# Preparing an output weight early, through memory, in an adaLN attention and gMLP kernel

## The chip, the cores and the metric

The kernel runs on one core of a Trainium2 chip. The metric is the time of one execution on the device in microseconds (us); of several runs the median counts. A core has five engines that work side by side, each through its own instructions in order: TensorE (PE, matrix products into the accumulators in PSUM; its weight loads are shown as PEld), VectorE (DVE), ScalarE (ACT), GpSimd (POOL) and SyncE (SP), which here only issues transfers between the chip's memory and the on-chip buffer SBUF. Transfers are carried out by 16 DMA engines. An engine or a queue that waits for something holds up all that stands behind it in its own order.

## The reference

A block with 2048 tokens of width 448, 16 heads of 28, and a hidden half-width of 896; all in float32:

```python
mod = (silu(c) @ w_mod).reshape(6, 448)          # sa, ca, ga, sb, cb, gb
h = layernorm(x) * (1 + ca) + sa
x = x + ga * attention(h, wqkv) @ wo             # 16 heads, softmax
h = layernorm(x) * (1 + cb) + sb
z = gelu(h @ w_in)                               # 2048 x 1792
z1, z2 = z[:, :896], layernorm(z[:, 896:])
g = w_sp @ z2 + b_sp[:, None]                    # mixing over the 2048 tokens
x = x + gb * ((z1 * g) @ w_out)                  # w_out: 896 x 448
```

The gate `gb` multiplies the columns of `w_out`'s result, so it can be multiplied into `w_out` beforehand.

## The kernel before

Matrix products that need more precision than one pass gives are done with operands split in two: a high part, which is the value rounded to the type float32r, and a low part, the value minus the high part. Three products (high by high, high by low, low by high) then stand for one. So each weight has to be split before it is used, one copy (high) and one subtraction (low) per block.

The work goes in stages: modulation, first layer norm and projections; attention; the attention's output projection and second layer norm; `z1` (first half of the hidden width, stored to memory); `z2`; mixing with the output projection laced into its end; the rest of the output projection.

**Attention.** A loop over 256 slots `u` (16 heads of 16 key blocks). Each slot issues four score matmuls and their exponentials (ScalarE), four matmuls for the row maxima of a later head (20 slots ahead) with their VectorE reductions, and, every other slot, the products with V of the two slots before. Side work is put into slots with `at(slot, fn, ...)`: in each slot first its events run in the order in which they were registered, then the matmuls, then the events in `late`. For each head there are loads of its q and k (`load_head`, SP, some 30 slots ahead of the head's first), the row of maxima (`m_fin`: ScalarE and GpSimd produce two rows, SP writes them into place; four slots before the head), and for finished heads the division and scatter of the result (`n_copy` to `n_scatter`). Other events prepare later work. `ws_load`, `ws_add` and `ws_store` form 80 sums of blocks of `w_sp` and store them, up to slot 187. `wo_load` and `wo_prep` do `wo`, from slot 120, with buffers of the pool `stage2` (two buffers under the tag `ql`). `win_first` loads half of `w_in` from slot 200.

**Mixing.** The product with `w_sp` is done with sums of blocks, in four phases p = 0 to 3 of two halves with eight steps each. A step is 21 matmuls in phases 0 to 2 and 12 in phase 3. For a step, `w_load` (SP, two to three steps ahead) loads one or two blocks of weights into `raw_sp` (four buffers), and `w_split` (one to two steps ahead) splits each: high part by ScalarE (L994), low part by VectorE (L84, the line of the helper `sub`). The matmuls are L1106 to L1108. At the end of each half, `evac` empties the accumulators with VectorE and ScalarE (L1112 is the VectorE addition). The function `extras(p, half, st)` adds the side work of a step; it is called one step later, after the loads and splits and ahead of the matmuls. The stationary operands of phases 0 to 2 lie in `heapA` (steps 0 to 3) and `heapB` (steps 4 to 7); those of phase 3 in `heapA` and the last columns of `heapB`, split from z2 by `prep3` (L1003).

**w_out.** Its seven blocks of 128 rows are prepared from step 3 of phase 2's second half to step 4 of phase 3's first half. `wout_load` loads a block into a buffer of the tag `x2t` (two buffers, L1189) and GpSimd multiplies it by the gate (L1190); `wout_part` makes the high part with ScalarE (L1194) and the low part with VectorE (L84), into the first 6272 columns of `heapB`, as these come free, and then calls `wout_load` for the block two further on. The output matmuls (`y_part`, L1212 to L1214) begin with the first step of phase 3's second half.

Of the kernel before, what the change touches and what calls it, by code (L numbers as in the profile page):

```python
# [8 lines left out]
F32 = mybir.dt.float32  # L9
F32R = mybir.dt.float32r  # L10
AF = mybir.ActivationFunctionType
ALU = mybir.AluOpType
# [4 lines left out]
S, D, H, DH, FH = 2048, 448, 16, 28, 896  # L17
# [16 lines left out]
def tile_adaln_mha_gmlp(ctx, tc, x, wqkv, wo, w_in, w_spT, b_sp, w_out, cT, w_mod, out):  # L34
    nc = tc.nc
    ctx.enter_context(tc.manual_schedule())
    pe, dve, act, pool, sp = nc.tensor, nc.vector, nc.scalar, nc.gpsimd, nc.sync
# [3 lines left out]
    scr = ctx.enter_context(tc.tile_pool(name="scr", bufs=1, space=DRAM))  # L41
# [4 lines left out]
    x2_scr = scr.tile([S, D], F32, name="x2_scr")  # L46
    z1_scr = scr.tile([FH, S], F32, name="z1_scr")
    ws_scr = scr.tile([80, 128, 512], F32, name="ws_scr")

    ident = const.tile([128, 128], F32, name="ident")  # L50
    make_identity(nc, ident)
# [8 lines left out]
    bcs = {"gb": const.tile([128, D], F32, name="bc_gb")}  # L60
# [5 lines left out]
    def hview(heap, off, a, b):  # L66
        return heap[:, off : off + a * b].rearrange("p (a b) -> p a b", b=b)
# [15 lines left out]
    def sub(eng, dst, a, hi):  # L83
        eng.tensor_tensor(out=dst, in0=a, in1=hi.bitcast(F32), op=ALU.subtract)  # L84
# [5 lines left out]
    def weight_part(dst, i, raw, hi_eng, lo_eng, zero=True, c0=0):  # L90

        cs = slice(c0, c0 + raw.shape[-1])
        h = dst[:, i if i < 3 else 6, cs]
        if hi_eng is act:
            act.activation(h, raw, AF.Copy)
        else:
            hi_eng.tensor_copy(h, raw)
        if i < 3:
            sub(lo_eng, dst[:, 3 + i, cs], raw, h)
        else:  # L100
            sub(lo_eng, dst[0:64, 7, cs], raw[0:64], h[0:64])
            if zero:
                pool.memset(dst[64:128, 7, cs].bitcast(F32), 0.0)
# [47 lines left out]
    stage2 = att.enter_context(tc.tile_pool(name="stage2", bufs=2, side="right"))  # L151
# [311 lines left out]
    for g in range(1, NG):  # L463
        if g == 3:
# [14 lines left out]
            def load_head(h, c0=0, c1=S):  # L479
                k, q = kst[h % 3], qst[h % 3]  # L480
                if h > 2:
                    sp.dma_start(q[84:86, :].bitcast(F32), q[86:88, :].bitcast(F32))
                for r0, i in ((0, 0), (56, 1), (28, 0)):
                    sp.dma_start(k[r0 : r0 + 28, c0:c1].bitcast(F32), qk_scr[i][D + h * DH : D + (h + 1) * DH, c0:c1])
                for r0, i in ((0, 0), (28, 1), (56, 0)):
                    sp.dma_start(q[r0 : r0 + 28, c0:c1].bitcast(F32), qk_scr[i][h * DH : (h + 1) * DH, c0:c1])
# [159 lines left out]
    def wo_prep(i):  # L646
        pool.tensor_tensor(out=wo_raw[i], in0=wo_raw[i], in1=bcs["ga"], op=ALU.mult)
        weight_part(wos, i, wo_raw.pop(i), pool, pool)

    wraw = []  # L650

    def win_first(i):
# [44 lines left out]
    def at(slot, fn, *a, when=events):  # L697
        when.setdefault(slot, []).append((fn, a))
# [20 lines left out]
    for i in range(4):  # L719
        at(120 + 8 * i, wo_load, i)  # L720
        at(124 + 8 * i, wo_prep, i)
        at(200 + 8 * i, win_first, i)

    load_head(1)

# [273 lines left out]
    def z_sum(dst, a, b, op=ALU.add, eng=pool):  # L999
        eng.tensor_tensor(out=dst, in0=a, in1=b, op=op)  # L1000
# [5 lines left out]
    def prep0(st):  # L1006
        h, l = zst[st][:, 0:896], zst[st][:, 896:1792]
        z_part(h[:, F1], l[:, F1], z2[st][:, F1])
        z_part(h[:, F2], l[:, F2], z2[8 + st][:, F1])
        z_part(h[:, F6], l[:, F6], z2[8 + st][:, F6])  # L1010

    def prep1(st):
        h, l = zst[st][:, 0:896], zst[st][:, 896:1792]
        z_part(h[:, F1], l[:, F1], z2[8 + st][:, F2])
        z_part(h[:, FQ], l[:, FQ], z2[st][:, FQ])

    def prep2(st):
        z_part(zst[st][:, 0:896], zst[st][:, 896:1792], z2[st])
# [44 lines left out]
    t4 = ctx.enter_context(tc.tile_pool(name="t4", bufs=2))  # L1063
# [14 lines left out]
    wouts_h, wouts_l = (hview(heapB, i * 3136, 7, D) for i in range(2))  # L1078
# [4 lines left out]
    def prep3(st):  # L1083
        a, b = z7[st]
        z_part(a[:, 0:384], a[:, 384:768], z2[8 + st][:, F1])
        z_part(b[:, 0:128], b[:, 128:256], z2[8 + st][:, F6])
# [66 lines left out]
    def z1_load():  # L1153
        if nz[0] < len(gates):
            f, tb = gates[nz[0]]
            if tb == 1:
                z1s[f, tb] = wp.tile([128, 512], F32, name="z1l", tag="raw_sp")
            else:
                z1s[f, tb] = t4.tile([128, 512], F32, name="z1")
            sp.dma_start(z1s[f, tb], z1_scr[f * 128 : (f + 1) * 128, tb * 512 : (tb + 1) * 512])  # L1160
            nz[0] += 1

    def b_load(tb):
        bt[tb] = t4.tile([128, 512], F32, name="bt")
        sp.dma_start(bt[tb], b_sp[tb * 512 : (tb + 1) * 512].rearrange("(o n) -> o n", o=1).broadcast_to([128, 512]))

    def gate(n=1):
        for _ in range(n):
            f, tb = gates[nz[1]]
            nz[1] += 1  # L1170
            u = utile(f, tb)
            d_add(u, u, bt[tb])
            d_add(u, u, z1s.pop((f, tb)), ALU.mult)
            z1_load()
# [3 lines left out]
    def u_split(f, tb):  # L1178
        if tb not in uTs:
            uTs[tb] = hview(dpool.tile([128, 8 * 896], F32R, name="uT", tag=f"heapD{tb % 2}"), 0, 14, 512)  # L1180
        uT, u = uTs[tb], utile(f, tb)
        act.activation(uT[:, f, :], u, AF.Copy)
        sub(dve, uT[:, 7 + f, :], u, uT[:, f, :])

    x2t, yps = {}, {}

    def wout_load(f):
        x2t["w", f] = raw = t4.tile([128, D], F32, name="raw_out", tag="x2t")
        sp.dma_start(raw, w_out[f * 128 : (f + 1) * 128, :])  # L1189
        pool.tensor_tensor(out=raw, in0=raw, in1=bcs["gb"], op=ALU.mult)  # L1190

    def wout_part(f):
        raw = x2t.pop(("w", f))
        act.activation(wouts_h[:, f, :], raw, AF.Copy)  # L1194
        sub(dve, wouts_l[:, f, :], raw, wouts_h[:, f, :])
        if f + 2 < 7:
            wout_load(f + 2)

    def x2_load(t):
        if 8 <= t < 12:  # L1200
            x2t[t] = t4.tile([128, D], F32, name="x2t")
        else:
            x2t[t] = wp.tile([128, 512], F32, name="x2l", tag="wsp_l")[:, :D]
        sp.dma_start(x2t[t], x2_scr[t * 128 : (t + 1) * 128, :])
# [15 lines left out]
    def extras(p, half, st):  # L1220
        if p == 0 and half == 0:
            if st < 2:
                prep0(6 + st)
            z_sum(z2[st][:, F2], z2[st][:, F2], z2[8 + st][:, F2], eng=dve)
        if p == 0 and half == 1:
            prep1(st)
        if p == 1 and half == 0:
            z_sum(z2[st][:, F1], z2[st][:, F1], z2[8 + st][:, F2])
            z_sum(z2[st][:, F2], z2[st][:, F2], z2[st][:, F1], ALU.subtract)
            z_sum(z2[8 + st][:, F1], z2[8 + st][:, F1], z2[st][:, F1], ALU.subtract)  # L1230
        if p == 1 and half == 1:
            prep2(st)
            if st == 6:
                b_load(2)
                b_load(3)
                z1_load()
                z1_load()
        if p == 2 and half == 0:
            if st < 6:
                gate()  # L1240
            if st > 4:
                u_split(st - 5, 2)
        if p == 2 and half == 1:
            for i in ((), (0,), (1,), (2, 3), (4, 5), (6,), (), (7,))[st]:
                prep3(i)
            if st in (1, 2, 3, 4):
                gate()
            if 3 <= st < 7:
                u_split(st, 2)
            if st in (3, 4):  # L1250
                wout_load(st - 3)
            if st > 5:
                wout_part(st - 6)
        if p == 3 and half == 0:
            if st < 5:
                wout_part(2 + st)
            if st == 6:
                x2_load(8)
            if st == 5:
                b_load(0)  # L1260
        if p == 3 and half == 1:
            if st < 4:
                gate()
            else:
                if st == 4:
                    b_load(1)
                u_split(st - 1, 3)
                gate(2 if st > 4 else 1)
            if st in (1, 2, 3):
                u_split(st - 1, 3)  # L1270

    nw = [4, 2]
    for n, (p, half, st) in enumerate(steps):
# [13 lines left out]
        if st == 7:  # L1287
            evac(p, half)
    extras(*steps[-1])
    z1_load()  # L1290
    z1_load()
# [44 lines left out]
```

## Time and profile before

| | |
|---|---|
| runs | 1409.55, 1411.18, 1412.63 us; median 1411.18 |
| profiled execution | 1410.07 us, span 1408.0 us, mean granted TensorE clock 1.000 |
| busy share | PE 99%, VectorE 72%, ScalarE 56%, GpSimd 20% |
| DMA | 186.99 MB, mean 133 GB/s |
| attention, from the first score matmul of the loop to the last (L566) | 153.8 to 872.4 us |
| mixing, from the first matmul start (L1106) to the last | 1060.9 to 1348.8 us |

The span runs from the first to the last instruction of the profiled execution. In the rows of the profile, "x <- y" after an operation names what it writes and reads, "x7" is a count of instructions, L is the line in the kernel, and a name in brackets or behind a bar with "<-" is what ended the engine's idle time before the instruction. "SPq" is SyncE's queue. In a timeline row the first number is the start and the second the length in us, and for several instructions in one row the length is that of them all.

### The profile page before, as it was taken

How to read it: one execution, taken by the hardware profiler on the slowest of the kernel's cores; microseconds unless marked ns; L12 is line 12 of the kernel's file. 1: busy time of each engine (PE TensorE's matmuls, PEld its weight loads, DVE VectorE, ACT ScalarE, POOL GpSimd, SP SyncE). 2: the span in 40 equal slices, each digit the busy share in tenths (PEclk: the TensorE clock that was granted, in tenths of full speed). 3: DMA queues.
4: the chain of work that ended last, by engine and by line, in shares of the span. 5: the costliest groups of instructions: out<-in, count | busy, mean ns of one | idle time of the engine just before them, and what ended most of it. 6: DMA issues, size and time to landing. Idle time of an engine off the chain costs nothing.

```text
span 1408.0 us, 20113 instructions
## 1 busy us (share of the span) xinstructions
PE 1393.6 (99%) x7180; PEld 979.8 (70%) x7180; DVE 1010.5 (72%) x1700; ACT 786.8 (56%) x1532; POOL 287.7 (20%) x276
## 2 busy tenths in 40 slices
PE   7999999999999999999999999999999999999998
PEld 6888655555555555555555554988998888887888
DVE  7778888888888888888888860751356655667573
ACT  3623677777677777777667779263234544334210
POOL 3033312221314243313200021100142430001000
PEclk9999999999999999999999999999999999999999
DMA  8564635555555556654422001534103333444453
GB/s 251 160 176 150 196 101 180 165 162 145 165 161 167 159 163 173 185 147 157 125 68 75 21 18 47 185 114 139 53 1 112 112 110 108 144 142 144 151 178 103
DMA packets 98251, 186.99 MB, mean 133 GB/s; under 512 B 16614, under 2 KB 28006, under 8 KB 95606
## 3 DMA queue, kind: packets, MB, share of 16 engines
q1 hardware_dynamic: 95722, 181.87, 42.7%
q10 hardware_dynamic: 2430, 3.84, 0.7%
q8 instruction: 56, 0.92, 0.3%
q14 instruction: 43, 0.35, 0.1%
HBM read 130.42 MB, written 50.45 MB: 128 GB/s over the span
## 4 chain that ended last, share of the span: by engine, by line
PE 93%; DVE 3%; DMA 2%; issue 1%; ACT 1%; POOL 1%; SPq 0%; ACTq 0%; DVEq 0%; POOLq 0%
PE st_ps L566 18%; PE o_ps L581 17%; PE mt L535 17%; PE acc L1107 6%; PE acc L1108 6%; PE acc L1106 6%; PE z_ps L1032 5%; PE z_ps L918 5%; PE pq L293 4%; PE wo_ps L788 3%; PE y_ps L1213 2%; PE y_ps L1212 2%; PE y_ps L1214 2%; PE pv L278 1%; DMA raw_sp<-ws_scr 1%
## 5 line engine op out<-in xcount | busy, mean ns | idle before, releaser
L540 DVE TENSOR_REDUCE pm<-mt 128x1 f32<-128x512 f32 x1024 | 631.4, 681 | 108.5 <-PE mt L535 108.3
L570 ACT ACTIVATE P<-st_ps 128x512 f32<-128x512 f32 x1024 | 512.5, 631 | 150.7 <-PE st_ps L566 150.7
L566 PE MATMUL st_ps<-qst,kst 128*128 128x512 f32 x1024 | 406.5, 408 | 0.5 <-ACT P L570 0.5
L535 PE MATMUL mt<-kst,qst 128*128 128x512 f32 x1024 | 402.6, 393 | 0.1
L566 PEld LDWEIGHTS st_ps<-qst,kst 128*128 128x128 f32 x1024 | 190.9, 187 | 153.7 <-issue 93.9
L581 PE MATMUL o_ps<-P,V 128*32 128x512 f32 x2048 | 247.5, 598 | 0.0
L535 PEld LDWEIGHTS mt<-kst,qst 128*128 128x128 f32 x1024 | 192.6, 188 | 30.7 <-DVE pm L540 2.3
L994 ACT ACTIVATE wsp_h<-raw_sp 128x512 fp32r<-128x512 f32 x112 | 70.2, 631 | 161.2 <-PE acc L1108 102.6
L688 POOL TENSOR_TENSOR ws_raw<-ws_raw 128x512 f32<-128x512 f32 x80 | 103.0, 1288 | 273.2 <-DMA ws_raw<-in_w_spT_dram 261.1
L84 DVE TENSOR_TENSOR wsp_l<-raw_sp,wsp_h 128x512 fp32r<-128x512 f32 x112 | 81.7, 738 | 90.2 <-ACT wsp_h L994 89.3
L581 PEld LDWEIGHTS o_ps<-P,V 128*32 128x32 f32 x2048 | 54.1, 109 | 123.6 <-issue 116.7
L1107 PE MATMUL acc<-wsp_l,heapA 128*128 128x512 f32 x224 | 87.3, 390 | 0.8 <-DVE wsp_l L84 0.8
L1106 PE MATMUL acc<-wsp_h,heapA 128*128 128x512 f32 x224 | 87.5, 390 | 0.2 <-DVE cD L1112 0.2
L1108 PE MATMUL acc<-wsp_h,heapA 128*128 128x512 f32 x224 | 87.2, 389 | 0.0
L1107 PE MATMUL acc<-wsp_l,heapB 128*128 128x512 f32 x174 | 67.7, 389 | 0.0
L1108 PE MATMUL acc<-wsp_h,heapB 128*128 128x512 f32 x174 | 67.7, 389 | 0.0
L1106 PE MATMUL acc<-wsp_h,heapB 128*128 128x512 f32 x174 | 67.7, 389 | 0.0
L293 PE MATMUL pq<-heapD,heapD 128*128 128x512 f32 x196 | 62.4, 392 | 0.0
L1036 DVE BATCH_NORM_STATS2 stz<-z 128x6 f32<-128x448 f32 x32 | 19.9, 625 | 50.4 <-ACT z L1035 29.5
L1106 PEld LDWEIGHTS acc<-wsp_h,heapA 128*128 128x128 f32 x224 | 42.0, 188 | 9.8 <-DVE cD L1112 1.2
L1107 PEld LDWEIGHTS acc<-wsp_l,heapA 128*128 128x128 f32 x224 | 42.0, 188 | 9.7 <-DVE wsp_l L84 1.2
L1108 PEld LDWEIGHTS acc<-wsp_h,heapA 128*128 128x128 f32 x224 | 42.1, 188 | 8.7
(205 smaller groups left out, 1593.7 us busy)
## 6 DMA issues: line engine op xcount, KB each, us to landing
ws_raw<-in_w_spT_dram SPq DMA_DIRECT2D x160, 256.0 KB
ws_scr<-ws_raw SPq DMA_DIRECT2D x80, 256.0 KB
raw_sp<-ws_scr SPq DMA_DIRECT2D x80, 256.0 KB
kst<-qk_scr SPq DMA_DIRECT2D x45, 224.0 KB
qst<-qk_scr SPq DMA_DIRECT2D x45, 224.0 KB
raw_sp<-in_w_spT_dram SPq DMA_DIRECT2D x32, 256.0 KB
qk_scr<-qh SPq DMA_DIRECT2D x28, 256.0 KB
qk_scr<-ql SPq DMA_DIRECT2D x28, 256.0 KB
```

What stands on the lines that cost most here:

```text
L84: eng.tensor_tensor(out=dst, in0=a, in1=hi.bitcast(F32), op=ALU.subtract)
L293: pe.matmul(pq, wqk[:, b, m * 128 : (m + 1) * 128], hT[g][:, a, :], start=j == 0, stop=j == NST - 1)
L535: pe.matmul(mt, qst[h % 3][:, t * 128 : (t + 1) * 128], kst[h % 3][:, kb * 512 : (kb + 1) * 512], start=True, stop=True)
L540: dve.tensor_reduce(out=pms[h][:, t, kb : kb + 1], in_=mt, axis=AX.X, op=ALU.max)
L566: pe.matmul(st, kst[h % 3][:, kt * 128 : (kt + 1) * 128], qst[h % 3][:, qb * 512 : (qb + 1) * 512], start=True, stop=True)
L570: act.activation(p, st, AF.Exp, scale=SCALE)
L581: pe.matmul(otile[h][32 * qb : 32 * qb + 32, :], V[:, kt, h, :], ptiles.pop((u, qb)), start=kt == 0, stop=kt == NT - 1)
L688: pool.tensor_tensor(out=a, in0=a, in1=b, op=SUMS[i // 16][2])
L918: pe.matmul(ps_t, w1[:, b, f * 128 : (f + 1) * 128], h2T[g][:, a, :], start=j == 0, stop=j == NST - 1)
L1106: pe.matmul(acc[i], zh, hi, start=st == 0, stop=False)
L1107: pe.matmul(acc[i], zh, lo, start=False, stop=False)
L1108: pe.matmul(acc[i], zl, hi, start=False, stop=st == 7)
```

## The change

The gate's multiplication and the split of `w_out` move into the attention's loop. For each of the seven blocks, from slot 196 on and six slots apart, SP loads the block into a buffer of `stage2`, three slots later GpSimd multiplies it by the gate, makes the high part with a copy and the low part with a subtraction, and two slots after that SP stores both parts to two arrays in memory. In the mixing, SP loads the 14 parts from there straight into their places in `heapB`, from step 6 of phase 2's second half to step 7 of phase 3's first half, one or two after each step. No other engine takes part there.

```diff
+    wout_scr = [scr.tile([FH, D], F32, name=f"wout_scr{i}") for i in range(2)]
...
+    wout_t = {}
+
+    def wout_raw(f):
+        wout_t[f] = stage2.tile([128, D], F32R, name="wout_l", tag="ql")
+        sp.dma_start(wout_t[f].bitcast(F32), w_out[f * 128 : (f + 1) * 128, :])
+
+    def wout_prep(f):
+        lo = wout_t[f]
+        hi = stage2.tile([128, D], F32R, name="wout_h", tag="ql")
+        pool.tensor_tensor(out=lo.bitcast(F32), in0=lo.bitcast(F32), in1=bcs["gb"], op=ALU.mult)
+        pool.tensor_copy(hi, lo.bitcast(F32))
+        sub(pool, lo, lo.bitcast(F32), hi)
+        wout_t[f] = hi, lo
+
+    def wout_store(f):
+        for scr_i, t in zip(wout_scr, wout_t.pop(f)):
+            sp.dma_start(scr_i[f * 128 : (f + 1) * 128, :], t.bitcast(F32))
...
+    for f in range(7):
+        at(196 + 6 * f, wout_raw, f)
+        at(199 + 6 * f, wout_prep, f)
+        at(201 + 6 * f, wout_store, f)
...
-    def wout_load(f):
-        x2t["w", f] = raw = t4.tile([128, D], F32, name="raw_out", tag="x2t")
-        sp.dma_start(raw, w_out[f * 128 : (f + 1) * 128, :])
-        pool.tensor_tensor(out=raw, in0=raw, in1=bcs["gb"], op=ALU.mult)
-
-    def wout_part(f):
-        raw = x2t.pop(("w", f))
-        act.activation(wouts_h[:, f, :], raw, AF.Copy)
-        sub(dve, wouts_l[:, f, :], raw, wouts_h[:, f, :])
-        if f + 2 < 7:
-            wout_load(f + 2)
+    wout_order = [(0, 0), (0, 1), (0, 2), (0, 3), (1, 0), (1, 1), (1, 2), (1, 3), (0, 4), (0, 5), (0, 6), (1, 4), (1, 5), (1, 6)]
+
+    def wout_load(n):
+        for i, f in wout_order[:n]:
+            sp.dma_start((wouts_h, wouts_l)[i][:, f, :].bitcast(F32), wout_scr[i][f * 128 : (f + 1) * 128, :])
+        del wout_order[:n]
...
-            if st in (3, 4):
-                wout_load(st - 3)
             if st > 5:
-                wout_part(st - 6)
+                wout_load(2)
         if p == 3 and half == 0:
-            if st < 5:
-                wout_part(2 + st)
+            wout_load(1 if st in (1, 2, 3, 4, 5, 6) else 2)
```

## Prediction, made before the changed kernel ran

> **What bounds the kernel now.** I read the page first: busy times, slices, chain of waits. Then the waits of TensorE (PE) alone, which say where it stands still at all; then the timeline around those places, engine by engine, and the waits of SP.
>
> ```profile
> span 1408.0 us, 20113 instructions
> PE 1393.6 (99%) x7180; PEld 979.8 (70%) x7180; DVE 1010.5 (72%) x1700; ACT 786.8 (56%) x1532; POOL 287.7 (20%) x276
> PE wu L220 <- DMA xg<-in_x_dram: 4.5, 1, 4.5
> PE tp L326 <- DVE xn L262: 2.7, 1, 2.7
> PE pv L278 <- DVE hfull L379: 1.4, 1, 1.4
> PE acc L1107 <- DVE wsp_l L84: 0.8, 1, 0.8
> PE st_ps L566 <- ACT P L570: 0.5, 1, 0.5
> PE acc L1106 <- DVE cD L1112: 0.2, 1, 0.2
> ```
>
> The columns of a wait are total us, times, longest. PE is busy 99% of the span, and the 14.4 us in which it isn't (1408.0 - 1393.6) bound what any change that leaves its matmuls alone can bring. The matmuls are left alone here. The first three waits belong to the kernel's start and to lines that the change doesn't touch; what is left for it is small: 0.8 and 0.2 us in the mixing, 0.5 us once in attention.
>
> **What the holes are worth.** Both waits of the mixing stand in the first steps of its last phase, exactly where w_out is prepared now. A wait's length leaves out the matmul stretched beside it, so I measure from start to start:
>
> ```profile
> 1289.41 0.39 PE L1108 MATMUL acc<-wsp_h,heapB 128*128 128x512 f32 x1
> 1289.63 0.39 PE L1106 MATMUL acc<-wsp_h,heapA 128*128 128x512 f32 x1
> 1290.82 0.39 PE L1108 MATMUL acc<-wsp_h,heapA 128*128 128x512 f32 x1
> 1291.44 0.50 PE L1106 MATMUL acc<-wsp_h,heapA 128*128 128x512 f32 x1 [0.24 <-DVE cD L1112]
> 1291.78 0.39 PE L1107 MATMUL acc<-wsp_l,heapA 128*128 128x512 f32 x1
> 1301.09 0.39 PE L1106 MATMUL acc<-wsp_h,heapA 128*128 128x512 f32 x1
> 1302.26 0.50 PE L1107 MATMUL acc<-wsp_l,heapA 128*128 128x512 f32 x1 [0.78 <-DVE wsp_l L84]
> 1302.60 0.39 PE L1108 MATMUL acc<-wsp_h,heapA 128*128 128x512 f32 x1
> ```
>
> The last phase begins at 1289.63 (heapA's turn), and an undisturbed start to start is 0.22 us (1289.41 to 1289.63). Hole A: 0.62 and 0.34 instead of 0.22 each, 0.52 us lost. Hole B: 1.17 and 0.34, 1.07 us lost. Together 1.6 us.
>
> **Part 1: removed from the mixing.** Per block of w_out: one load of 224 KB (SP), one GpSimd multiply, one ScalarE copy, one VectorE subtraction, seven times.
>
> ```profile
> L1190 POOL TENSOR_TENSOR raw_out<-raw_out,bc_gb x7: 1144/1155/1499, 1279.4 to 1307.5; 128x448 f32<-128x448 f32 x7
> L1194 ACT ACTIVATE heapB<-raw_out x7: 561/562/581, 1286.4 to 1309.1; 128x448 fp32r<-128x448 f32 x7
> L84 DVE TENSOR_TENSOR heapB<-raw_out,heapB x7: 611/615/618, 1287.2 to 1309.8; 128x448 fp32r<-128x448 f32 x7
> SPq L1189 <- DVE heapB L84: 17.1, 3, 7.0
> ```
>
> That is 8.5 us of GpSimd, 3.9 of ScalarE, 4.3 of VectorE: beside a PE that is full, worth nothing in themselves. What counts is the order on two queues.
>
> ```profile
> 1287.18 0.62 DVE L84 TENSOR_TENSOR heapB<-raw_out,heapB 128x448 fp32r<-128x448 f32 x1
> 1287.65 0.51 ACT L1003 ACTIVATE heapB<-z 128x384 fp32r<-128x384 f32 x1
> 1287.72 0.68 DVE L1112 TENSOR_TENSOR cE<-cE,acc 128x512 f32<-128x512 f32 x1
> 1295.61 0.33 SPq L1189 DMA_DIRECT2D raw_out<-in_w_out_dram  x1
> 1296.05 1.23 SPq L986 DMA_DIRECT2D raw_sp<-ws_scr  x1
> 1299.88 0.63 ACT L994 ACTIVATE wsp_h<-raw_sp 128x512 fp32r<-128x512 f32 x1 [7.67 <-DMA raw_sp<-ws_scr]
> 1300.51 1.15 POOL L1190 TENSOR_TENSOR raw_out<-raw_out,bc_gb 128x448 f32<-128x448 f32 x1 [0.79 <-DMA raw_out<-in_w_out_dram]
> 1300.55 1.65 DVE L84 TENSOR_TENSOR wsp_l<-raw_sp,wsp_h 128x512 fp32r<-128x512 f32 x1 [3.82 <-ACT wsp_h L994]
> L84 DVE TENSOR_TENSOR wsp_l<-raw_sp,wsp_h x14: 676/692/1654, 1269.3 to 1309.2; 128x512 fp32r<-128x512 f32 x14
> ```
>
> Hole A: PE waits for a PSUM bank that VectorE's evacuation (L1112, from 1287.72) has not emptied. The subtraction for w_out's first block stands right ahead of it in VectorE's order, from start to start 0.54 us. Without it the evacuation moves up by 0.54, the hole's 0.52 closes. It could move further only if the split ahead of it did.
>
> Hole B has two causes in a row. SP sat on wout_load until VectorE freed raw_out's buffer (17.1 us in three waits, one of 7.0), and the mixing weights' own load (raw_sp, L986) stood behind it until 1296.05; it reached ScalarE at 1299.88, which had idled 7.67 us for it. Then VectorE's subtraction took 1.65 us beside GpSimd's multiply, which began 0.04 us before it; the median of the 14 such rows around is 0.69, so 0.96 too long. Either cause alone nearly makes the hole. Both go: the new loads write heapB and need no VectorE or GpSimd, only that the old phase's matmuls have read those columns. Waits go by columns, not by the whole buffer: ScalarE writes heapB (L1003) at 1287.65, while PE reads other columns of it up to 1289.41. The columns of the first four high parts were last read in step 4 of the old phase's second half; three steps of 21 matmuls at 0.23 follow it, so it ended 14 us before 1289.6, near 1275, and SP gets to these loads at about 1282. So SP is held by raw_sp's own buffers only, and I cost the waits of the new loads at nothing; were they held to the end of that phase (1289.6), the next raw_sp would land 4.2 us later (ScalarE's 1284.65 behind SP's 1280.49, below) and be split in 0.63 + 0.69, by 1295.2, and the step that needs it, the fourth of the phase, begins at 1298.4 (one step, 12 x 0.22, ahead of 1301.09): still nothing.
>
> What made that row 1.65 us long could speak against the change, which moves GpSimd's work beside another VectorE stage. The Trainium skill, SBUF — State Buffer, section "SBUF: two separate sides", says GpSimd and a two-input VectorE instruction on SBUF exclude each other for a whole instruction. The 1.65 us row agrees. By that rule VectorE's attention work, which reads PSUM, is not held and the sum stays -1.6. The Trainium skill, Perfetto Trace Analysis, section "Optimizing Scalar/DVE Operations", warns without that limit that moving work between the two may not help; by it the third rival below would hold.
>
> **Part 2: added to the mixing.** Fourteen loads of 224 KB instead of seven, 3.2 MB (14 x 229 KB in decimal) for 1.6. Issue on SP: 14 x 0.33 us by L1189's row above, 4.6 us for 2.3, in a queue that mostly waits. Traffic:
>
> ```profile
> 1280.00:1285.00 5.00, 5.00 (x24) 4.14 (x23) 3.62 (x6) 2.74 (x6) 1.66 (x2) 1.00 0.76 255
> 1280.49 1.59 SPq L986 DMA_DIRECT2D raw_sp<-ws_scr  x3
> 1284.65 1.29 ACT L994 ACTIVATE wsp_h<-raw_sp 128x512 fp32r<-128x512 f32 x2 [2.17 <-DMA raw_sp<-ws_scr]
> ```
>
> The first row's columns: stretch, its length, busy PE, PEld, DVE, ACT, POOL (instructions), granted clock, DMA share, GB/s. The clock is full and 255 GB/s pass. A last-phase step is 12 matmuls, 2.7 us; one raw_sp (262 KB) and one w_out part (229 KB) per step are 182 GB/s, so the queue keeps up. The tightest place is the three raw_sp issued at 1280.49, which VectorE must split ahead of the evacuation. Today a w_out load goes just ahead of them (1.02 MB, 4.0 us at 255, ScalarE started after 4.16). In the new kernel that one is gone and two follow: 1.25 MB if all share alike, 4.9 us, with an issue some 0.5 us earlier. Bounds on hole A: from closed (in order) to an evacuation 0.9 - 0.5 = 0.4 us later for this and 0.54 earlier for the subtraction, 0.14 in all, so 0.38 of the 0.52 left. I take closed, since the loads are issued in order. The last two parts are issued ahead of the second half's first step, and the output matmuls that read them come after 36 matmuls, 7.9 us, even if SP runs no further ahead than PE; a load takes 4.2: nothing.
>
> **Part 3: added to attention.** Per block on GpSimd a multiply, a copy, a subtraction; on SP one load and two stores.
>
> ```profile
> L647 POOL TENSOR_TENSOR wo_raw<-wo_raw,bc_ga 128x448 f32<-128x448 f32 x4 | 4.6, 1143 | 0.0
> L628 POOL CAST heapD<-heapD 128x512 fp32r<-128x512 f32 x12 | 7.3, 611 | 2.3 <-DMA heapD<-osb 2.3
> sum 140.00, PE 140.00 PEld 78.64 DVE 114.79 ACT 101.69 POOL 9.50; mean PE 15.56 PEld 8.74 DVE 12.75 ACT 11.30 POOL 1.06
> L540 DVE TENSOR_REDUCE pm<-mt x1024: 624/680/693, 90.9 to 833.8; 128x1 f32<-128x512 f32 x171
> L688 POOL TENSOR_TENSOR ws_raw<-ws_raw 128x512 f32<-128x512 f32 x80 | 103.0, 1288 | 273.2 <-DMA ws_raw<-in_w_spT_dram 261.1 <-PE st_ps L566 11.9
> SPq L684 <- DMA ws_scr<-ws_raw: 134.6, 55, 5.1
> 710.93 0.63 SPq L593 DMA_DIRECT2D rt<-osb  x1
> 757.12 0.63 SPq L593 DMA_DIRECT2D rt<-osb  x1
> ```
>
> 7 x (1.14 + 0.61 + 1.14) = 20.2 us of GpSimd, the subtraction priced as the multiply; the sum row is 700 to 840 us, where the new slots fall, and GpSimd is busy 9.5 of 140. SP issues 21 transfers and twice waits per block (each store for GpSimd, each reload of the buffer for the store before it). The same pattern (load, GpSimd, store, reload of the buffer) ran 80 times earlier (L688): SP waited 134.6 us there, 5.1 at the longest, with no wait of PE behind it. What stands behind: head loads, the scatter, and the row of maxima of the next head (L559), which has four slots of 2.9 us (757.12 - 710.93 is a head's 16 slots), 11.5 us, until its first score matmul. A wout_prep of 2.9 us or a 5.1 us wait ahead of it fits. Cost 0; if one such wait came through whole, 5.1 us, the upper end.
>
> **Sum**, against the profiled execution (1410.07 us, span 1408.0): -0.52 - 1.07 = -1.6, 1408.5. That execution lies 1.1 under the median of 1411.18, whose runs spread over 3.1 us; from the median, 1409.6.
>
> **Rivals.** First, nothing moves: the holes close, but a later one opens by as much, or hole A stays and B shrinks to what a late raw_sp leaves. Against it: everything after 1303 waits for PE, not PE for it (waits above). 1411.2. Second, slower: a w_out part keeps SP or the queues from raw_sp in each of the last phase's steps, as hole B does once. It decides when raw_sp is issued less than 5.5 us (4.2 + 0.63 + 0.69) ahead of its step. Seven steps of 1.07 give +7.5, 1418.7. Against it: raw_sp leads by two steps or more, and the rate fits. Third, slower: the 21 GpSimd instructions each lengthen a VectorE reduction in attention by 0.96, 20 us, and PE waits for all of it: 1430. It decides where VectorE's idle 25 us of 140 no longer take it up. Against it: no reduction of 1024 took more than 693 ns, beside 80 GpSimd additions. Fourth, more than 2.8 us faster, 1408.3 or less: there is no such idle time of PE beyond the start, so only the runs' spread could show it.
>
> **How the numbers follow.** 0.2%, 2.8 us, is what a measurement of this kernel can tell from no change. Forecast (1.1 to 1.6 us gained: hole B, and A in part or whole) 0.75, no gain 0.14, second rival 0.05, third 0.02, fourth 0.04. Range: the forecast and no gain, each with the runs' half spread of 1.5 (1409.6 - 1.5 and 1411.2 + 1.5): 1408.1 to 1412.7. Faster 0.05, same 0.88, slower 0.07.
>
> **What would show it.** Right: no PE wait between 1285 and 1310, wsp_l's longest subtraction there at 0.69 instead of 1.65, ScalarE's 7.67 us wait for raw_sp gone, L1189's waits gone from SP, GpSimd empty around them; in attention reductions still at 0.68 and some 20 us more GpSimd at 720 to 830. Wrong: PE waiting for wsp_l again in the last phase, with SP on the w_out parts ahead of it (second rival); reductions above 0.7 us (third); a wait of st_ps after a head's change (SP in attention); hole A still there, with ScalarE later than 1284.2 at the split ahead of the evacuation.

## The result and the profile after

The changed kernel takes 1409.27 us in the median of 21 runs (1407.93 to 1413.70), the kernel before 1411.48 in the median of 21 beside it (1409.55 to 1412.88). The ratio is 0.9987, 95% interval 0.9981 to 0.9993: by the ratio 1.8 us faster, between 1.0 and 2.7, and so below the 0.2% that the prediction counted as a change. The profiled execution of the changed kernel took 1409.25 us, its span 1407.4.

From the page of the changed kernel, its first lines:

```profile
span 1407.4 us, 20172 instructions
PE 1395.1 (99%) x7180; PEld 982.2 (70%) x7180; DVE 1006.2 (71%) x1693; ACT 783.6 (56%) x1525; POOL 296.4 (21%) x290
```

VectorE and ScalarE lose seven instructions each, GpSimd has 14 more (seven multiplies moved, seven copies and seven subtractions new). PE's busy time is 1.5 us longer than before (1395.1 against 1393.6) with the same 7180 matmuls and a shorter span: it also counts what a matmul takes longer, which differs between these two executions (below). The waits of PE over the whole span (total us, times, longest):

```profile
PE wu L221 <- DVE st L252: 4.9, 1, 4.9
PE pv L279 <- DVE hfull L380: 1.4, 1, 1.4
PE tp L327 <- DVE xn L263: 1.2, 1, 1.2
PE st_ps L567 <- ACT P L571: 0.5, 1, 0.5
PE tp L118 <- DVE ql L85: 0.2, 1, 0.2
```

Both waits of the mixing are gone. The stretches where the holes were (columns as in the prediction):

```profile
1285.00:1290.00 5.00, 5.00 (x23) 4.14 (x23) 2.95 (x5) 2.67 (x5) 0.00 (x0) 1.00 1.02 377
1290.00:1295.00 5.00, 5.00 (x23) 4.14 (x23) 5.00 (x10) 1.44 (x4) 0.00 (x0) 1.00 0.59 218
1295.00:1300.00 5.00, 5.00 (x23) 4.13 (x22) 3.18 (x7) 0.82 (x2) 0.00 (x0) 1.00 0.48 147
1300.00:1305.00 5.00, 5.00 (x23) 4.13 (x22) 1.38 (x2) 1.26 (x2) 0.00 (x0) 1.00 0.89 264
```

PE is full in each, GpSimd empty. In this execution the last phase starts at 1291.63. On VectorE's timeline the evacuation (L1135, L1112 before) now stands right behind the split of uT:

```profile
1288.35 0.69 DVE L85 TENSOR_TENSOR uT<-cF,uT 128x512 fp32r<-128x512 f32 x1
1288.95 0.68 DVE L1135 TENSOR_TENSOR cE<-cE,acc 128x512 f32<-128x512 f32 x1
```

It begins 2.68 us ahead of the phase's start, 1.91 before (1289.63 - 1287.72): 0.77 earlier, of which 0.54 is the subtraction that is gone. SP's timeline (L1009 loads the mixing's weights, L1214 the parts of w_out):

```profile
1282.02 1.33 SPq L1009 DMA_DIRECT2D raw_sp<-ws_scr  x3
1283.40 0.90 SPq L1214 DMA_DIRECT2D heapB<-wout_scr  x2
1284.39 0.38 SPq L1009 DMA_DIRECT2D raw_sp<-ws_scr  x1
1284.83 0.92 SPq L1214 DMA_DIRECT2D heapB<-wout_scr  x2
1287.38 0.32 SPq L1009 DMA_DIRECT2D raw_sp<-ws_scr  x1
```

The fifth of these weight blocks, the one for the phase's fifth step, is issued 4.2 us ahead of the phase's start; before, it was issued 6.4 us behind it (1296.05 against 1289.63). ScalarE waits at most 2.8 us for such a block between 1285 and 1310 us, where it had waited 7.67. What SP itself waits for in 1270 to 1310 us, with the weights for their buffers and with the new loads for PE:

```profile
SPq L1009 <- DVE wsp_l L85: 8.4, 5, 6.0
SPq L1214 <- PE acc L1131: 0.6, 3, 0.2
SPq L1214 <- PE acc L1130: 0.3, 1, 0.3
```

VectorE's subtractions for the weights in 1270 to 1312 us, and what GpSimd now does in attention (rows by tile, duration ns min/median/max):

```profile
L85 DVE TENSOR_TENSOR wsp_l<-raw_sp,wsp_h x16: 684/692/694, 1272.0 to 1308.8; 128x512 fp32r<-128x512 f32 x16
```

```profile
L660 POOL TENSOR_TENSOR wout_l<-wout_l,bc_gb x7: 1138/1144/1161, 724.1 to 824.2; 128x448 f32<-128x448 f32 x7
L661 POOL CAST wout_h<-wout_l x7: 556/557/563, 725.4 to 825.5; 128x448 fp32r<-128x448 f32 x7
L85 POOL TENSOR_TENSOR wout_l<-wout_l,wout_h x7: 1140/1152/1157, 726.0 to 826.1; 128x448 fp32r<-128x448 f32 x7
```

**One profile against one profile misleads here.** The two spans differ by 0.6 us, the two medians by 2.2. Followed by stages, first the score matmuls of attention and the output matmuls (before, then after):

```profile
L566 PE MATMUL st_ps<-qst,kst x1024: 387/393/507, 153.8 to 872.4; 128*128 128x512 f32 x171
L1212 PE MATMUL y_ps<-heapB,uT x112: 362/368/369, 1315.8 to 1403.5; 128*128 128x448 f32 x112
```

```profile
L567 PE MATMUL st_ps<-qst,kst x1024: 387/395/504, 154.6 to 874.4; 128*128 128x512 f32 x171
L1230 PE MATMUL y_ps<-heapB,uT x112: 362/365/369, 1316.1 to 1402.9; 128*128 128x448 f32 x112
```

| stretch | before | after | difference |
|---|---|---|---|
| span's start to the first score matmul | 153.8 | 154.6 | +0.8 |
| first to last score matmul | 718.6 | 719.8 | +1.2 |
| last score matmul to the last phase's start | 417.2 | 417.2 | 0 |
| last phase's start to the first output matmul | 26.14 | 24.48 | -1.66 |
| first to last output matmul (L1212, L1230) | 87.7 | 86.8 | -0.9 |

Only the fourth row is the change. The first row goes with the clock granted to TensorE in the first 40 us (the columns as in the prediction; the kernel before, the changed kernel, and the kernel before profiled again, which is run below):

```profile
0.00:40.00 40.00, 31.37 (x178) 28.30 (x179) 31.38 (x72) 18.64 (x36) 11.17 (x18) 1.00 0.90 252
0.00:40.00 40.00, 32.53 (x173) 29.41 (x174) 30.38 (x70) 17.91 (x35) 10.99 (x18) 0.96 0.88 245
0.00:40.00 40.00, 31.49 (x150) 28.75 (x151) 26.79 (x62) 13.45 (x29) 10.89 (x18) 0.83 0.76 219
```

At 1.00, 0.96 and 0.83 the first score matmul starts at 153.8, 154.6 and 159.1 us. The change doesn't touch this stretch, and the same kernel showed 1.00 and 0.83. The second and the fifth row were open: a cost in attention, and a gain that nobody had forecast, each about as large as what was sought. The experiments settle that neither is the change's.

### The profile page after: what moved, and what is told of

The parts are those of the page before. It is cut to its first block, busy times and chain, and to the rows that moved or that the text cites. A ratio compares the mean times of both kernels' runs of the same rounds, so it can differ in the third digit from the quotient of the medians.

```text
span 1407.4 us, 20172 instructions
## 1 busy us (share of the span) xinstructions
PE 1395.1 (99%) x7180; PEld 982.2 (70%) x7180; DVE 1006.2 (71%) x1693; ACT 783.6 (56%) x1525; POOL 296.4 (21%) x290
## 4 chain that ended last, share of the span: by engine, by line
PE 96%; DVE 2%; DMA 1%; ACT 1%; issue 0%; POOL 0%; SPq 0%; DVEq 0%; ACTq 0%; POOLq 0%
PE st_ps L567 18%; PE o_ps L582 17%; PE mt L536 17%; PE acc L1129 6%; PE acc L1131 6%; PE acc L1130 6%; PE z_ps L1055 5%; PE z_ps L941 5%; PE pq L294 4%; PE wo_ps L811 3%; PE pv L279 2%; PE y_ps L1231 2%; PE y_ps L1232 2%; PE y_ps L1230 2%; DMA wm<-in_w_mod_dram 1%; PE tp L118 0%
```

## The experiments

The holes below are measured as in the prediction, from start to start of matmuls, less 0.227 us for each undisturbed one. "To first output" is the fourth row of the table above.

| kernel | hole A | hole B | to first output | ratio to before, 95% |
|---|---|---|---|---|
| before | 0.55 | 1.06 | 26.14 | 1 |
| before, profiled again | 0.56 | none | 25.14 | |
| attention half alone | 0.63 | 0.82 | 25.98 | 1.0004 (0.9995 to 1.0013) |
| no multiply | 0.60 | 0.21 | 25.55 | 0.9999 (0.9991 to 1.0008) |
| parts of w_out a step later | 0.06 | 1.02 | 26.10 | 1.0002 (0.9993 to 1.0010) |
| before, early uT | 0.49 | 1.14 | 26.23 | 1.0001 (0.9992 to 1.0010) |
| after | none | none | 24.48 | 0.9987 (0.9981 to 0.9993) |
| after, profiled again | none | none | 24.48 | |
| after, GpSimd beside the splits | 0.46 | none | 24.98 | 0.9994 (0.9985 to 1.0003) |
| after, GpSimd thrice in attention | none | none | 24.48 | 0.9986 (0.9975 to 0.9997) |
| after, loads at the phase's end | none | none | 24.48 | 0.9988 (0.9979 to 0.9997) |
| after, early uT | none | none | 24.48 | 0.9984 (0.9975 to 0.9992) |

**The attention half alone.** The kernel before, with `wout_raw`, `wout_prep` and `wout_store` and their slots as in the change:

```diff
+    for f in range(7):
+        at(196 + 6 * f, wout_raw, f)
+        at(199 + 6 * f, wout_prep, f)
+        at(201 + 6 * f, wout_store, f)
```

> The kernel before, with the attention half of the change alone: the seven blocks are gated, split and stored between slots 196 and 237, and nobody reads them; the mixing prepares w_out as before. Theory (all of the gain is in the mixing, the attention half is free): time as before, 1411.5 within 0.7 us; holes A (0.52 us lost) and B (1.07) both there, 1.6 in all from start to start. Rival 1 (the attention half costs what the changed kernel's profile lost in attention, 719.8 us instead of 718.6 from the first to the last score matmul): about 1.2 us slower than before. Rival 2 (the gain comes from something in attention): faster than before by 1 us or more.

1411.15 us against 1411.35. The score matmuls take 718.9 us from first to last, and both holes are there (waits of PE):

```profile
PE acc L1130 <- DVE wsp_l L85: 0.5, 1, 0.5
...
PE acc L1129 <- DVE cD L1135: 0.2, 1, 0.2
```

The attention half costs nothing that the interval (-0.7 to +1.8 us) or the profile shows, and it gains nothing: the gain lies in the mixing.

**No multiply.** The kernel before without GpSimd in the mixing (the gate is then left out of the result):

```diff
         sp.dma_start(raw, w_out[f * 128 : (f + 1) * 128, :])
-        pool.tensor_tensor(out=raw, in0=raw, in1=bcs["gb"], op=ALU.mult)
```

> The kernel before without GpSimd's multiply in the mixing; the gate gb is left out of the computation. SP is still held by the w_out buffers. Theory (hole B needs both causes): wsp_l's subtractions all at 0.69 us, hole B shrinks from 1.07 us to 0.1 to 0.2, hole A stays at 0.5; about 0.9 us faster than before. Rival (SP's hold alone makes hole B): hole B stays at 0.8 to 1.1, time as before.

VectorE's subtractions for the weights, in 1270 to 1312 us:

```profile
L84 DVE TENSOR_TENSOR wsp_l<-raw_sp,wsp_h x15: 683/693/694, 1269.5 to 1311.3; 128x512 fp32r<-128x512 f32 x15
```

The 1.65 us row is gone and hole B with it, but for 0.21 us (another 0.16 us is lost 17.5 us into the phase); hole A stays. SP still holds the weights back as before, so its hold alone makes only a fifth of hole B. The time (1410.54 against 1411.35 in the median, ratio undecided) can't resolve 0.8 us.

**GpSimd beside the splits.** The changed kernel, with a multiply beside seven of the splits:

```diff
             for raw in raws.pop(n):
+                if 50 <= n < 57:
+                    dead = t4.tile([128, D], F32, name="dead", tag="x2t")
+                    pool.tensor_tensor(out=dead, in0=raw[:, :D], in1=bcs["gb"], op=ALU.mult)
```

> The changed kernel with seven GpSimd multiplies of 128x448 put beside the splits of seven of the last phase's weight blocks (each reads the block as it lands and writes a buffer that nobody reads). SP is not held. Theory (GpSimd alone makes no hole, since the splits now run steps ahead of PE): wsp_l's subtractions there rise from 0.69 to 1.1 to 1.65 us in most of the seven rows, no PE wait longer than 0.25 us, time as the changed kernel, 1409.3 within 0.7. Rival (GpSimd's port alone makes hole B): a PE wait on wsp_l of 0.5 us or more, 1 us slower than the changed kernel.

From GpSimd's and VectorE's timelines; the phase starts at 1291.59:

```profile
1287.37 1.15 POOL L1018 TENSOR_TENSOR dead<-raw_sp,bc_gb 128x448 f32<-128x448 f32 x1 [140.43 <-DMA raw_sp<-ws_scr]
```

```profile
1287.69 1.38 DVE L85 TENSOR_TENSOR wsp_l<-raw_sp,wsp_h 128x512 fp32r<-128x512 f32 x1 [0.46 <-ACT wsp_h L1020]
1288.99 0.68 DVE L85 TENSOR_TENSOR uT<-cF,uT 128x512 fp32r<-128x512 f32 x1
1289.60 0.68 DVE L1138 TENSOR_TENSOR cE<-cE,acc 128x512 f32<-128x512 f32 x1
...
1301.84 1.07 DVE L85 TENSOR_TENSOR wsp_l<-raw_sp,wsp_h 128x512 fp32r<-128x512 f32 x1 [2.76 <-ACT wsp_h L1020]
```

Hole B does not come: with the weights early, a long subtraction (1.07 us at 1301.84) is covered. But only two of the rows are long, fewer than expected, because the splits run at other times than the blocks land. And hole A comes back, 0.46 us, which no theory expected: one GpSimd instruction makes the split ahead of the evacuation 1.38 us long, and the evacuation begins 1.99 us ahead of the phase instead of 2.68. Whatever stands there, a subtraction of w_out or a lengthened one, makes the hole.

**Parts of w_out a step later.** The kernel before, with the copy and the subtraction of each block one mixing step later:

```diff
-            if st > 5:
-                wout_part(st - 6)
+            if st > 6:
+                wout_part(st - 7)
...
-            if st < 5:
-                wout_part(2 + st)
+            if st < 6:
+                wout_part(1 + st)
```

> The kernel before with each of the seven copy-and-subtract steps for w_out one mixing step later, so that none of them stands ahead of VectorE's evacuation at the phase's end. Theory (hole A is that subtraction): the evacuation starts 0.54 us earlier against the phase's start, hole A closes (0.52 to 0.1 or less); hole B stays between 0.5 and 1.5 us, since SP is still held and GpSimd still multiplies. Time 0.5 us below before if B is as large, which the runs hardly resolve: the holes in the trace decide. Rival (hole A comes from a late weight block ahead of the evacuation): hole A stays at 0.4 or more.

From PE's timeline; the phase starts at 1292.33:

```profile
1304.42 0.50 PE L1107 MATMUL acc<-wsp_l,heapA 128*128 128x512 f32 x1 [0.75 <-DVE wsp_l L84]
...
1317.62 0.50 PE L1106 MATMUL acc<-wsp_h,heapA 128*128 128x512 f32 x1 [0.21 <-DVE cE L1112]
```

Hole A closes (0.06 left). The evacuation begins 2.42 us ahead of the phase instead of 1.91, with the splits of the weights ahead of it where they were (4.30 and 3.63 us ahead of the phase, 4.31 and 3.66 before), so it was that subtraction and not a late weight block. Another hole opens at the next evacuation, 25 us into the phase: 0.49 us are lost at 1317.6. From VectorE's timeline:

```profile
1314.78 0.62 DVE L84 TENSOR_TENSOR heapB<-raw_out,heapB 128x448 fp32r<-128x448 f32 x1
1316.28 0.69 DVE L84 TENSOR_TENSOR wsp_l<-raw_sp,wsp_h 128x512 fp32r<-128x512 f32 x1 [0.89 <-ACT wsp_h L994]
1316.89 1.87 DVE L1112 TENSOR_TENSOR cE<-cE,acc 128x512 f32<-128x512 f32 x3
```

The last subtraction for w_out is over before VectorE idles 0.89 us. What stands right ahead of this evacuation is the split of a late weight block: ScalarE had waited 0.98 us for its load, and SP had been held by w_out's last block until 1310.14. By these rows the hole comes from SP's order, as the first cause of hole B does. The time does not move.

**GpSimd thrice in attention.** The changed kernel, with two more rounds of two-input operations and a copy per block:

```diff
+        for _ in range(2):
+            pool.tensor_tensor(out=hi, in0=lo.bitcast(F32), in1=bcs["gb"], op=ALU.mult)
+            pool.tensor_tensor(out=hi, in0=lo.bitcast(F32), in1=bcs["gb"], op=ALU.mult)
+            pool.tensor_copy(hi, lo.bitcast(F32))
         pool.tensor_copy(hi, lo.bitcast(F32))
```

> The changed kernel with GpSimd's work per block in attention about tripled (four more two-input operations and two more copies per block, overwritten by the real ones): some 60 us of GpSimd instead of 20. Theory (free, since the reductions read PSUM and GpSimd has room): reductions still at 0.68 us, no new PE wait, 1409.3 within 0.7. Rival (GpSimd's work holds VectorE or the next head's row of maxima): if the first 20 us cost 1 us, 40 more cost 2, and reductions above 0.7 us or a PE wait on st_ps show it.

1408.55 us against 1411.06, just under the expected band. Attention's stretch (columns as above), and VectorE's reductions:

```profile
150.00:875.00 725.00, 724.48 (x4047) 408.01 (x4047) 584.97 (x982) 528.86 (x1073) 225.73 (x213) 1.00 0.47 139
```

```profile
L541 DVE TENSOR_REDUCE pm<-mt x1024: 626/682/694, 91.9 to 834.8; 128x1 f32<-128x512 f32 x171
```

GpSimd is busy 226 us there, 40 more than in the changed kernel (185.6), and PE, the reductions and the time are where they were. Its work beside this VectorE work is free.

**All in one slot.** The changed kernel, with load, preparation and store of a block in the same slot:

```diff
-        at(196 + 6 * f, wout_raw, f)
-        at(199 + 6 * f, wout_prep, f)
-        at(201 + 6 * f, wout_store, f)
+        at(210 + f, wout_raw, f)
+        at(210 + f, wout_prep, f)
+        at(210 + f, wout_store, f)
```

> The changed kernel with load, preparation and store of a block all in one slot, seven blocks in slots 210 to 216. SP then sits out each load, GpSimd's 2.9 us and each store: some 10 us per block, 70 us in all, with the next head's transfers behind it. Theory (what makes the attention half free is that its SP waits are spread over 42 slots): SP reaches the next head's row of maxima (slot 220) some 70 us after slot 210, where its scores start 40 us after; PE waits 25 to 40 us and the kernel is that much slower, about 1440. Rival (SP's waits don't matter in attention): time as the changed kernel.

1433.95 us in the median of two runs, 22.9 more than before and 24.7 more than the changed kernel. The first of PE's waits, and SP's issue of the first block's load and of the row of maxima:

```profile
PE st_ps L567 <- DMA qst<-nl: 23.4, 1, 23.4
```

```profile
762.91 0.38 SPq L655 DMA_DIRECT2D wout_l<-in_w_out_dram  x1
...
821.48 0.56 SPq L560 DMA_DIRECT2D qst<-nh  x1
```

SP needs 58.6 us for the seven blocks, some 8 each, and a few transfers among them, and the next head's row of maxima stands behind: one wait of 23.4 us, nearly the whole loss, and a little shorter than the 25 to 40 expected. Part of the rest follows the wait: the granted clock is 0.50 from 804 to 828 us, and the first matmuls after it run 0.43 us from start to start instead of 0.23. The attention half is free because its waits are spread over slots, not because SP has nothing to do. In the changed kernel SP waits only this much for the stores there (715 to 840 us), and 2.2 us for GpSimd's two parts:

```profile
SPq L655 <- DMA wout_scr<-wout_h: 8.1, 4, 4.8
```

**All loads at once, twice.** In the first kernel `wout_load(14)` was called in place of the first `wout_load(2)`, ahead of the old phase's last step:

> The changed kernel with all 14 loads of w_out issued in one go, at step 6 of the old phase's second half, so that SP is held by the last columns of heapB until the old phase has ended, and the weight block for the fourth step of the last phase is issued only then, behind 3.2 MB. Theory (slack of some 3 us is left even then): that block lands about 4.5 us after the phase's start, is split by 6, needed at 8.2; no PE wait over 0.25 us, time as the changed kernel. Rival (loads of w_out ahead of the weights open a new hole): a PE wait on wsp_h or wsp_l of 0.5 us or more within 14 us of the phase's start.

It took 1419.32 us against 1411.06, and PE waited for the loads themselves:

```profile
PE acc L1129 <- DMA heapB<-wout_scr: 8.2, 1, 8.2
```

This tests something else than was meant. The last parts go to columns of `heapB` from which that last step still reads its operand, and in the program they now stand ahead of it; so it waits for them, and reads w_out's parts in the operand's place. It shows the price of placing such a load one step too early and says nothing of the queue. The price is more than the wait: from the last score matmul to the last phase's start it is 427.2 us instead of 417.2, since the granted clock is 0.51 from 1290 to 1297 us and the matmuls behind the wait run 0.43 us from start to start instead of 0.23. The second kernel calls it one step later:

```diff
-            if st > 5:
-                wout_load(2)
+            if st == 7:
+                wout_load(14)
...
-            wout_load(1 if st in (1, 2, 3, 4, 5, 6) else 2)
```

> The changed kernel with all 14 loads of w_out in one go behind the weight block for the fourth step of the last phase, after the old phase's last matmuls in the program; SP is held by the last columns until that phase has ended, and the block for the fifth step is issued only then, behind 3.2 MB. Theory (there is room for that): issued about 0.3 us after the phase's start, landed by 5, split by 6.3, needed at 10.9; no PE wait over 0.25 us, time as the changed kernel, 1409.3 within 0.7. Rival (w_out's parts ahead of the weights open a new hole, the second rival of the prediction): a PE wait on wsp_h or wsp_l of 0.5 us or more within 14 us of the phase's start.

1408.65 us against 1410.56, and PE waits for nothing between 1280 and 1400 us. From SP's timeline; the phase starts at 1292.25:

```profile
1284.73 7.92 SPq L1214 DMA_DIRECT2D heapB<-wout_scr  x14
1292.94 7.28 SPq L1009 DMA_DIRECT2D raw_sp<-ws_scr  x6
```

The next weight block is issued 0.7 us behind the phase's start, behind all 3.2 MB, and still no hole opens. The prediction's second rival asked for a block issued less than 5.5 us ahead of its step; this one, for the fifth step, is issued 10 us ahead of it, so even with the whole traffic in front that condition isn't reached.

**Early uT, twice.** On the kernel before and on the changed one, the last split of the fourth token block moves up one step:

```diff
-                u_split(st - 1, 3)
+                for f in ((3,), (4,), (5, 6), ())[st - 4]:
+                    u_split(f, 3)
```

> The kernel before with the last split of the fourth token block's operand (uT, block 6) one step earlier, so that the first output matmuls after the mixing don't wait for it. In the kernel before, PE lost 0.1 us there and then kept a start-to-start distance of 0.2067 us to the end; in the changed kernel, after the same wait, 0.2031: 0.9 us over 260 matmuls. Theory (the pace is set by how the matmuls start again after a wait): without the wait the pace stays at 0.2026 as ahead of it, and the last matmul comes 0.9 to 1.0 us earlier against the mixing's end; about 1.0 us faster than before. Rival (the pace differs from execution to execution, whatever the wait, or belongs to how w_out came into heapB): pace at 0.2067, time as before.

> The changed kernel with the last uT split one step earlier, as in the run on the kernel before. There is no wait of PE left in the mixing's second part. Theory: the wait of 0.1 us at the first output matmuls after the mixing is gone and the pace to the end is 0.2027 us instead of 0.2031, 0.1 us over 260 matmuls; 0.2 us faster than the changed kernel, which the runs can't tell from it (1409.1 within 0.7), and 1.8 to 2 us faster than before. Rival (the earlier split takes ScalarE's and VectorE's time from the step it moves to and opens a hole there): a PE wait of 0.25 us or more in the last eight steps.

The wait of 0.1 us goes in both, and the pace of the last 261 output matmuls is 0.2027 us. The first kernel's time, however, is 1411.03 us against 1411.06, not 1 us less; the profiles again (below) suggest why: the slow pace doesn't come with every execution. The second takes 1408.68 us against 1410.56, the lowest ratio of all here, 0.9984; whether it beats the changed kernel (0.9987) stays open, since the intervals overlap nearly whole.

**Both kernels again.** Nothing edited, one profile each; the two executions took 1414.56 and 1409.12 us.

> The kernel before, unchanged, for a second profiled execution. If the slow pace of the last output matmuls (0.2067 us from start to start in the first profile of this kernel and in that with the attention half added, 0.2031 in the others that wait there) belongs to the kernel's own timing, it is 0.2067 again. If it differs from execution to execution, it may be 0.2031 here. The holes, 1.6 us together, are there either way.

> The changed kernel, unchanged, for a second profiled execution. Attention's 719.8 us from the first to the last score matmul (718.6 before; 718.7 to 718.9 in the four runs with GpSimd's work there that have been looked at) is execution noise if it is near 718.7 here, a cost of the change if it is 719.5 or more. No holes; the pace of the last output matmuls 0.2031 if it goes with the kernel.

The kernel before, its output matmuls, and GpSimd and VectorE around the place of hole B:

```profile
L1212 PE MATMUL y_ps<-heapB,uT x112: 362/365/369, 1321.2 to 1408.0; 128*128 128x448 f32 x112
```

```profile
1306.50 1.37 POOL L1190 TENSOR_TENSOR raw_out<-raw_out,bc_gb 128x448 f32<-128x448 f32 x1 [0.58 <-DMA raw_out<-in_w_out_dram]
```

```profile
1306.17 0.69 DVE L84 TENSOR_TENSOR wsp_l<-raw_sp,wsp_h 128x512 fp32r<-128x512 f32 x1 [3.01 <-ACT wsp_h L994]
1306.78 1.57 DVE L84 TENSOR_TENSOR heapB<-raw_out,heapB 128x448 fp32r<-128x448 f32 x1
```

Three answers. The kernel before took 4.5 us longer than in its first profile, and its first score matmul starts 5.3 us later, at the low granted clock shown above. The pace of the output matmuls is the fast one here, 0.2031, in the very same kernel, so the 0.9 us in the table's last row belong to the execution. And hole B is not there: the late weight block reached VectorE 0.33 us ahead of GpSimd's start instead of 0.04 behind it, its subtraction took 0.69 us, and the long row fell on the next instruction, for which nobody waits. The block also reached VectorE earlier against the phase, 10.11 us behind its start, where the four profiles with the hole have 10.43 to 11.03; this profile doesn't separate the two. The expectation that both holes are there either way failed. The changed kernel again:

```profile
L567 PE MATMUL st_ps<-qst,kst x1024: 387/393/507, 155.6 to 874.3; 128*128 128x512 f32 x171
```

718.7 us from first to last, 719.8 in its first profile; the kernel before shows 718.6 and, profiled again, 719.8. The 1.2 us in attention are no cost of the change: of the 1.1 us between the changed kernel's two profiles, 0.8 had built up by the 700th of the 1024 score matmuls, before GpSimd's new work begins at 724.1 us.

## Why the prediction was right, point by point

**The sum.** Forecast 1409.6 from the median of three, measured 1409.27; forecast -1.6, measured -1.8 (-2.7 to -1.0). Sorted by mean granted clock (0.995 to 1.000), the changed kernel's 21 runs lie 0.8 to 2.9 us below the 79 runs of the kernel before that went beside the experiments, at each of the five values, so the clock doesn't account for the gain. Against the profiles alone, the stretch with the holes gave -1.66, and -0.66 against the kernel before profiled again: that the forecast came so near is in part luck (hole B, below). That the spans differ by 0.6 only is made of +2.0 up to attention's end and -0.9 in the output matmuls, both seen to change between executions of one kernel. For the same reason the 14.4 us that the prediction called a bound are not a strict one: what a matmul takes longer counts as busy.

**Hole A.** As forecast: it was the subtraction ahead of the evacuation (closed when that moved, and back at 0.46 us when the split ahead of the evacuation was lengthened instead). The evacuation came 0.77 us earlier, not 0.54, because the splits ahead of it came earlier too. The upper bound (0.38 us of it left if the loads share the queue alike) didn't come: with two loads right behind, the split ahead of the evacuation started 5.6 us before the phase (1286.00), 0.65 earlier than before.

**Hole B.** The place, the two causes and the size in that execution were right; one step was not. "Either cause alone nearly makes the hole" fell: SP's hold alone left 0.21 us, GpSimd alone none. It takes both, and a race between two transfers for which comes first: in the four profiles with the hole GpSimd's multiply began 0.04 to 0.09 us ahead of the split, in the fifth 0.33 behind it. Of five profiles with the old mixing and the multiply, four show a hole of 0.82 to 1.14 us and one none, so the term was sized from one throw: 0.8 us is the mean of the five, not 1.07. With hole A's 0.55 that is 1.35 us instead of 1.6; the measured interval holds both.

**The waits of the new loads.** Right: SP waited for PE's columns 0.9 us in all (L1214), and the weights ran ahead until their buffers, not the queue, held them.

**Attention.** Cost 0 was right: the half alone made no difference, and three times the GpSimd work neither. GpSimd's work was 7 x (1.14 + 0.56 + 1.15) = 20 us, forecast 20.2. SP's wait for a store was 4.8 us at the longest, within the 5.1 taken as a bound. The third rival (reductions lengthened) is refuted at 60 us of GpSimd: no reduction of 1024 over 694 ns. The Trainium skill, SBUF — State Buffer, section "SBUF: two separate sides", lets VectorE instructions with two inputs in SBUF (or in a two-port mode) and GpSimd exclude each other, and no others of VectorE. The rows agree on both sides of it: 1.38 to 1.66 us for such subtractions that start just after a GpSimd multiply, no change for reductions of PSUM. The wider warning of the Trainium skill, Perfetto Trace Analysis, section "Optimizing Scalar/DVE Operations", did not hold here, beside VectorE work that reads PSUM.

**What stays open.** The runs tell the changed kernel from the one before by 1.8 us, but not 0.5 from 1.0, so the shares of A and B in the time rest on the traces. The mean of the holes seen, 1.35 us, and the measured 1.8 agree within the interval; what the 0.45 us between them is, if anything, stays open.

## What to carry to other kernels

When PE is 99% busy, list its own waits first: their sum, measured from start to start, is what moving work off the other engines could bring here, whatever that work's busy time. A preparation step costs by what stands behind it in its engine's or queue's order (an evacuation, the next weights), so move it to where its waits are spread and nothing with a deadline stands behind. Before a difference of 1 us between two profiles is explained, profile one of the kernels again: here attention's length, the last matmuls' pace and one of the two holes all changed by about that much with nothing edited.

## What the runs showed of the hardware

The output matmuls of 448 columns run at one of two steady paces after a wait of 0.1 us: 0.2031 us from start to start in most profiles, 0.2067 in two (the kernel before, and that with the attention half), held for 260 matmuls, 0.9 us in all; without the wait 0.2027 in both kernels. What chooses between them was not found: the same kernel showed both, and the same distance of 0.31 us from start to start preceded both. One thing goes with it: those two profiles are the only ones with this wait in which the granted clock never fell to a half before the kernel's end; in the ten others it did, in nine near the start and in one at 1290 us. That it is the cause isn't shown.

The granted clock falls to 0.5 for 0 to 14 us within the first 30 us, differently from execution to execution, and the first score matmul starts at 153 to 154 us without it and at 158 to 159 us with the longest such stretch. It also fell to 0.5 in the two long waits of PE (23.4 and 8.2 us), and the first matmuls after them ran 0.43 us from start to start.

Attention's 718.6 to 718.9 us or 719.6 to 719.8 us from first to last score matmul are likewise two lengths that came with either kernel. The transfers started within 5 us of the changed kernel make 377 GB/s (with a DMA share of 1.02, so a little of it ran on past the stretch), well above the 255 from which the prediction bounded the crowding of the queue.
